# A new order for the 1254 hand-numbered steps of an attention, Fourier and feed-forward kernel

## The chip, the core and the metric

The kernel runs on one core of a Trainium2 chip, in one launch. The metric is the device time of one execution in microseconds (us). Five engines work side by side, each through its own instructions in a fixed order: TensorE (PE; its weight loads are listed as PEld), VectorE (DVE), ScalarE (ACT), GpSimd (POOL) and SyncE (SP). In this kernel SP issues every DMA. An instruction starts when the one ahead of it on its engine has started or ended and the semaphores that it waits for are set, so an instruction that waits holds up everything behind it on that engine.

## The reference

```python
# q, k, v: (4 batches, 12 heads, 448 tokens, 64), float32
scores = cap * np.tanh(q @ k.T / sqrt(64) / cap)        # cap = 30
attn   = exp(scores - max) / (sum(exp(scores - max)) + 1e-9)
x      = (attn @ v), heads side by side: (4, 448, 768)
mixed  = real(fft(fft(x, axis=1), axis=2))              # tokens, then features
u      = x + mixed
un     = (u - mean(u)) / sqrt(var(u) + 1e-6)            # over the 768 features
out    = u + maximum(un @ w_ch1, 0) @ w_ch2             # 768 -> 3072 -> 768
```

## The kernel before, in words

The program is written as small steps, one Python function each; every step issues a handful of instructions. The table `ORDER` gives each step of the first part a number from 1 to 1254, the steps are sorted by it (`at`, `plan.sort`) and issued in that order. Each engine gets its share of that list in the same sequence; the framework puts in the semaphores. So the table sets the order on every engine, SP among them, and nothing reorders it later. A step may not stand ahead of what it needs.

The steps, by what they do:

- **Attention, 48 heads in 24 pairs.** `load_qk` (two DMAs into one of three `qkr` buffers) and `load_v` (into one half of `vt`). `split_q` (DVE) and `split_k` (ACT) round to the high part, `rest_q` and `rest_k` (DVE) make the rest. `scores` (4 or 6 matmuls, L435) fills one of two PSUM tiles `s`; `tanh` (ACT, L445) empties it into one of four tiles `a`; `exp` (ACT, L448) works in place; `weigh` (8 matmuls, L465) multiplies by v. There are 84 tiles of scores and 168 `weigh`. After the seventh `weigh` of a pair, `denominators` and `normalise` (DVE, L479 to L486) put the result into `u`.
- **Fourier transform, once per batch** (`transform`). `fold_tokens`, `fold_features`, `fold_rest` (DVE) and `fold_split` (ACT) use symmetry; `stage1` (12 matmuls, `yps`, L532), `split_y` (ACT), `rest_y` (DVE), `stage2` (18 matmuls, `pq`, L556), `add_u` (DVE, L577 and L581).
- **Layer norm, once per batch.** `moments` (DVE, L590, L591), `rows` (ten small POOL instructions, L599 to L608), `standardise` (four on ACT, L623), `u_cols` (transposes on PE, `pt`, L632), `u_copy` (ACT, into `xc`). `rows_out` (four DMAs, L615) writes two numbers per token to DRAM, four bytes at a time; `row` reads them back over all partitions, for `residual` (DVE).
- **Feed-forward.** `fetch` (DMA) and `weights` (ACT and DVE, three steps a half chunk) make the weights from float64. `operand` (ACT) and `operand_rest` (DVE) split `xc`. A `product` is 6 matmuls: `up` (`ph`, L754, with relu on ACT at every third) or `down` (`po`, L783, added to `xc` by DVE, L792). The hidden layer is worked in 12 groups of 256; the first group (48 products) stands in the table, the other eleven follow in a fixed loop behind it that is not changed.
- **Constants.** `load_constant` and `constant` bring in the cosines and sines.

PSUM tiles `yps`, `pq`, `pt` and every second `po` share two buffers (tag "d"); `av` and the other `po` share one. Here is how a step finds its place:

```python
        i = number[name] = number.get(name, -1) + 1
        t = ORDER[name][i]
        plan.append((t, len(plan), key, f, args, needs))
```

Of the kernel before, what the change touches and what calls it, by code (L numbers as in the profile page):

```python
# [86 lines left out]
        327, 344, 355, 367, 605, 609, 633, 643, 872, 874, 902, 908, 1123, 1126, 1134, 1137  # L87
    ],
    "constant": [
        154, 152, 105, 99, 57, 55, 13, 12  # L90
    ],
    "denominators": [
        60, 103, 148, 185, 236, 280, 338, 375, 411, 473, 517, 558, 619, 651, 691, 743, 791, 828, 891, 918,
        964, 1018, 1055, 1092
    ],
    "exp": [
# [5 lines left out]
    ],  # L102
    "fetch": [
        10, 11, 56, 101, 222, 261, 283, 398, 494, 496, 992, 1007, 1113, 1115
    ],
    "fold_features": [
        158, 161, 195, 198, 291, 294, 437, 440, 489, 493, 569, 572, 687, 689, 753, 756, 839, 841, 929, 932,
        1042, 1045, 1102, 1103
    ],
    "fold_rest": [  # L110
        171, 174, 206, 215, 301, 304, 452, 453, 503, 506, 579, 582, 698, 708, 762, 767, 847, 850, 939, 943,
        1050, 1052, 1106, 1107
    ],
    "fold_split": [
        166, 169, 201, 210, 297, 300, 447, 450, 498, 501, 574, 578, 695, 703, 758, 761, 843, 846, 935, 937,
        1047, 1049, 1104, 1105
    ],
    "fold_tokens": [
        116, 121, 191, 193, 286, 288, 430, 434, 478, 485, 564, 567, 672, 684, 748, 750, 834, 837, 924, 927,
        1031, 1040, 1099, 1101  # L120
    ],
    "load_cap": [
        1
    ],
    "load_constant": [
        108, 104, 61, 59, 15, 14, 3, 2
    ],
    "load_qk": [
        4, 5, 6, 21, 29, 37, 72, 82, 90, 123, 133, 149, 172, 184, 212, 242, 253, 277, 309, 329, 345, 368, 395,
        438, 443, 487, 500, 522, 534, 552, 586, 606, 625, 644, 673, 709, 717, 759, 775, 789, 804, 821, 856,  # L130
        871, 887, 903, 966, 988
    ],
    "load_v": [
        7, 8, 54, 100, 146, 190, 237, 279, 337, 372, 446, 492, 516, 559, 618, 650, 713, 764, 793, 829, 889,
        917, 972, 1017
    ],
    "moments": [
        350, 353, 379, 383, 624, 629, 657, 661, 877, 886, 914, 934, 1127, 1131, 1139, 1140
    ],
    "normalise": [  # L140
        62, 63, 107, 110, 150, 151, 186, 189, 241, 243, 281, 284, 340, 341, 377, 378, 412, 414, 474, 475, 521,
        524, 561, 562, 620, 621, 654, 656, 693, 696, 744, 747, 792, 796, 830, 831, 892, 894, 921, 922, 969,
        976, 1019, 1025, 1065, 1066, 1093, 1098
    ],
    "operand": [
        604, 607, 1067, 1073, 1076, 1091, 1129, 1130, 1132, 1133, 1135, 1136, 999, 1021, 1062, 1190, 1191,
        1192, 1170, 1183, 1193, 1195, 1197, 1198
    ],
    "operand_rest": [
        716, 719, 1071, 1077, 1080, 1094, 1155, 1157, 1159, 1161, 1166, 1169, 1074, 1081, 1084, 1211, 1213,  # L150
        1214, 1231, 1232, 1234, 1235, 1237, 1238
    ],
    "product": [
# [90 lines left out]
    ],  # L244
# [765 lines left out]
```

## Time and profile before

| | us |
|---|---|
| time, median of 3 runs (1073.27 to 1073.58) | 1073.48 |
| span of the profiled execution, first to last instruction | 1064.8 |
| what lies around the span (1073.48 less 1064.8) | 8.7 |
| PE busy | 1017.9 |
| DVE busy | 795.8 |
| ACT busy | 403.9 |
| first matmul starts | 8.5 |
| first group of the feed-forward ends (step 1254) | 415 |

The page gives no total of its own for the profiled execution beyond the span; the 8.7 us are what the timed runs have more. A busy PE is not a PE at its peak: a matmul that streams at half clock is as busy. So the stretches below are read with the column of the granted clock beside the busy time: 1.00 is 2.4 GHz, and 0.50 is 1.2 GHz.

### The profile page before, as it was taken

How to read it: one execution, taken by the hardware profiler on the slowest of the kernel's cores; microseconds unless marked ns; L12 is line 12 of the kernel's file. 1: busy time of each engine (PE TensorE's matmuls, PEld its weight loads, DVE VectorE, ACT ScalarE, POOL GpSimd, SP SyncE). 2: the span in 40 equal slices, each digit the busy share in tenths (PEclk: the TensorE clock that was granted, in tenths of full speed). 3: DMA queues.
4: the chain of work that ended last, by engine and by line, in shares of the span. 5: the costliest groups of instructions: out<-in, count | busy, mean ns of one | idle time of the engine just before them, and what ended most of it. 6: DMA issues, size and time to landing. Idle time of an engine off the chain costs nothing.

```text
span 1064.8 us, 15143 instructions
## 1 busy us (share of the span) xinstructions
PE 1017.9 (96%) x5856; PEld 944.6 (89%) x5856; DVE 795.8 (75%) x1581; ACT 403.9 (38%) x626; POOL 19.2 (2%) x50
## 2 busy tenths in 40 slices
PE   6999899899978789999999999999999999999998
PEld 5899899899877678999999999999999999999997
DVE  5888778668685877777878888787778777777833
ACT  6997797796781411212122221222121222212200
POOL 0000100200100100000000000000000000000000
PEclk9999899999888999999999999999999999999999
DMA  8654763683521010121212212112122122121123
GB/s 222 166 140 108 106 130 87 83 120 94 57 43 47 9 39 17 58 66 48 68 51 62 60 45 69 56 49 60 46 60 60 45 60 59 46 60 54 37 80 129
DMA packets 59239, 77.02 MB, mean 72 GB/s; under 512 B 35616, under 2 KB 40736, under 8 KB 59168
## 3 DMA queue, kind: packets, MB, share of 16 engines
q1 hardware_dynamic: 59168, 76.06, 30.2%
q8 instruction: 46, 0.75, 0.3%
q14 instruction: 25, 0.20, 0.1%
HBM read 70.53 MB, written 5.52 MB: 71 GB/s over the span
## 4 chain that ended last, share of the span: by engine, by line
PE 87%; DVE 4%; ACT 3%; POOL 2%; DMA 2%; issue 1%; SPq 1%; POOLq 0%; ACTq 0%; DVEq 0%
PE ph L754 33%; PE po L783 32%; PE av L465 10%; PE s L435 6%; PE yps L532 3%; PE pq L556 2%; DMA raw<-w1r 1%; ACT u L623 1%; PE pt L632 1%; DVE bs L590 1%; ACT a L445 1%; DVE xc L792 1%; POOL ln L601 0%; DMA qkr<-qkT 0%; SPq L615 0%
## 5 line engine op out<-in xcount | busy, mean ns | idle before, releaser
L783 PE MATMUL po<-hh,w 128*128 128x448 f32 x1728 | 362.9, 368 | 4.5 <-DVE u L577 2.0
L754 PE MATMUL ph<-xs,w 128*128 128x448 f32 x1728 | 359.4, 366 | 3.3 <-DVE xs L327 2.6
L783 PEld LDWEIGHTS po<-hh,w 128*128 128x128 f32 x1728 | 324.6, 189 | 36.6 <-DVE xc L792 4.9
L754 PEld LDWEIGHTS ph<-xs,w 128*128 128x128 f32 x1728 | 323.9, 188 | 31.0 <-DVE xs L327 3.4
L792 DVE TENSOR_TENSOR xc<-xc,po 128x448 f32<-128x448 f32 x288 | 177.2, 618 | 47.3 <-PE po L783 45.4
L465 PEld LDWEIGHTS av<-vt,a 128*114 128x114 f32 x1344 | 153.4, 183 | 8.9 <-ACT a L445 2.0
L465 PE MATMUL av<-vt,a 128*114 128x65 f32 (+1 forms) x1344 | 153.8, 269 | 4.4 <-DVE u L486 1.6
L766 DVE SCALAR_TENSOR_TENSOR hh<-ph,hh 128x448 fp32r<-128x448 f32 x96 | 60.0, 625 | 114.3 <-ACT hh L765 114.3
L667 ACT ACTIVATE wt<-raw 128x384 f32<-128x384 f32 x96 | 53.1, 553 | 229.2 <-DVE w L699 224.7
L765 ACT ACTIVATE hh<-ph 128x448 fp32r<-128x448 f32 x96 | 52.3, 545 | 200.0 <-PE ph L754 200.0
L435 PE MATMUL s<-qhl,khl 128*128 128x452 f32 x384 | 101.6, 399 | 14.0 <-DVE qhl L327 8.5
L322 ACT CAST w<-wt 128x384 fp32r<-128x384 f32 x96 | 48.9, 509 | 121.5 <-DVE wt L674 120.7
L448 ACT ACTIVATE a<-a,capt 128x904 f32<-128x904 f32 x84 | 88.3, 1051 | 1.8
L445 ACT ACTIVATE a<-s,tscale 128x904 f32<-128x904 f32 x84 | 84.6, 1007 | 11.5 <-PE s L435 9.2
L435 PEld LDWEIGHTS s<-qhl,khl 128*128 128x128 f32 x384 | 70.9, 200 | 19.9 <-ACT khl L322 8.5
L674 DVE SCALAR_TENSOR_TENSOR wt<-wt 128x384 f32<-128x384 f32 x96 | 53.6, 558 | 18.3 <-ACT wt L667 8.8
L327 DVE TENSOR_TENSOR wt<-wt,w 128x384 f32<-128x384 f32 x96 | 52.9, 551 | 7.8 <-ACT w L322 7.8
L671 DVE SCALAR_TENSOR_TENSOR wt<-raw,wt 128x384 uint32<-128x384 uint32 x96 | 53.6, 558 | 3.3
L693 DVE SCALAR_TENSOR_TENSOR wt<-raw,wt 128x384 f32<-128x384 uint32 x96 | 53.6, 558 | 3.3
L699 DVE TENSOR_TENSOR w<-wt 128x384 fp32r<-128x384 f32 x96 | 53.6, 558 | 3.4
L532 PE MATMUL yps<-seqT,f 113*128 113x226 f32 (+1 forms) x288 | 38.4, 289 | 4.0 <-DVE f L327 4.0
L532 PEld LDWEIGHTS yps<-seqT,f 113*128 113x128 f32 (+1 forms) x288 | 36.7, 203 | 4.6 <-DVE f L327 4.4
(64 smaller groups left out, 544.9 us busy)
## 6 DMA issues: line engine op xcount, KB each, us to landing
qkr<-qkT SPq DMA_DIRECT2D x96, 226.0 KB, 3.9
raw<-w2r SPq DMA_DIRECT2D x48, 384.0 KB, 3.2
raw<-w1r SPq DMA_DIRECT2D x48, 384.0 KB, 3.1
vt<-vr SPq DMA_DIRECT2D x24, 288.0 KB, 4.4
outT<-xc SPq DMA_DIRECT2D x24, 224.0 KB, 1.9
fraw<-feat SPq DMA_DIRECT2D x6, 193.0 KB, 5.0
dev<-lnrow SPq DMA_DIRECT2D x4, 224.0 KB, 9.5
mean<-lnrow SPq DMA_DIRECT2D x4, 224.0 KB, 3.4
```

Source lines behind the costliest of these rows:

```text
L435: nc.tensor.matmul(ps_t[t][:, i, :SQ], khl[j][:, n, k0 : k0 + P], qhl[:, j], start=((n, j) == terms[0]), stop=((n, j) == terms[-1]),)
L445: nc.scalar.activation(a_t[t], ps_t.pop(t)[:, :, :SQ], AF.Tanh, scale=tscale)
L448: nc.scalar.activation(a_t[t], a_t[t], AF.Exp, scale=capt)
L465: nc.tensor.matmul(pa_t[p][:R, g // 2, o : o + n_ * (D + 1)], a_t[t][:, n, OFF[g] : OFF[g] + R], v, start=u % 7 == 0 and g % 2 == 0, stop= ...
L532: nc.tensor.matmul(ps[:, n * NT2 : (n + 1) * NT2], f[:cnt, ia, 2 * n + c], seqT[n][:cnt, ib, c], start=(k_ == 0), stop=(k_ == 5),)
L671: nc.vector.scalar_tensor_tensor(tu, hi.bitcast(U32), 0xC0000000, tu, op0=ALU.bitwise_and, op1=ALU.bitwise_or)
L674: nc.vector.scalar_tensor_tensor(t, w, HI_MIN, t, op0=ALU.is_ge, op1=mul)
L693: nc.vector.scalar_tensor_tensor(w, lo, 2.0**-52, w, op0=mul, op1=mul)
L754: nc.tensor.matmul(ph[:, :S], w_[:, dc * P : (dc + 1) * P], x_, start=(k_ == 0), stop=(k_ == 3 * NDC - 1),)
L766: nc.vector.scalar_tensor_tensor(hh[:, 1], ph[:, :S], 0.0, f32(hh[:, 0]), op0=ALU.max, op1=sub)
L783: nc.tensor.matmul(po[:, :S], w_[:, dc * P : (dc + 1) * P], hh[:, x_], start=(k_ == 0), stop=(k_ == 3 * GF - 1),)
L792: nc.vector.tensor_tensor(ac, ac, po[:, :S], op=add)
```

## The change

Only the table is changed: each of the 1254 steps gets a new number. No step is added or dropped, no instruction changes its shape, and the loop behind the table is the same. The first list of the table and one that moves far:

```diff
     "load_constant": [
-        108, 104, 61, 59, 15, 14, 3, 2
+        251, 78, 201, 90, 160, 80, 110, 31
     ],
     "rows_out": [
-        402, 404, 449, 457, 677, 680, 722, 728, 946, 949, 975, 994, 1146, 1148, 1164, 1178
+        536, 790, 811, 858, 726, 727, 865, 866, 947, 959, 1007, 1011, 1135, 1137, 1197, 1209
     ],
```

Since the table is written on two lines fewer, every line of the changed kernel behind it has a number lower by two (L435 becomes L433). Three places show what moves.

First, ACT at the start of the program. `khl` is the split keys, `seqT` and `featT` are constants, `a` a tile of scores, `guard` a small constant that needs `cap`. Before:

```order
L362 ACT_TABLE_LOAD
L362 ACTIVATE guard<-ncap 128x1
L322 CAST seqT<-sraw 128x452
L322 CAST featT<-fraw 128x386
L322 CAST khl<-qkr 128x448 x2
L445 ACTIVATE a<-s,tscale 128x904
L448 ACTIVATE a<-a,capt 128x904
```

Now, with what each row waits for:

```order
L320 ACT_TABLE_LOAD [waits DMAHW1_49]
L320 CAST khl<-qkr 128x448 [waits DMAHW0_49]
L360 ACTIVATE guard<-ncap 128x1 [waits DVE_49]
L320 CAST khl<-qkr 128x448 [waits DMAHW4_49,DMAHW3_49]
L443 ACTIVATE a<-s,tscale 128x904 [waits PE_49]
L446 ACTIVATE a<-a,capt 128x904 [waits DMAHW2_49,Activation_49]
```

The two constants left the head of the queue, and the table load, which waited for nothing, now waits for a DMA: the second half of the first head's queries and keys.

Second, ACT around the layer norm of batch 0. `u<-u,ln` is `standardise`, `xc<-pt` is `u_copy`, `a` are the tanh and exp of later scores. Before:

```order
L322 CAST khl<-qkr 128x448
L623 ACTIVATE u<-u,ln 114x768 x4
L322 CAST khl<-qkr 128x448
L667 ACTIVATE wt<-raw 128x384
L322 COPY xc<-pt 128x448 x2
L445 ACTIVATE a<-s,tscale 128x904
L322 COPY xc<-pt 128x448 x2
L448 ACTIVATE a<-a,capt 128x904
L322 COPY xc<-pt 128x448 x2
```

Now:

```order
L621 ACTIVATE u<-u,ln 114x768
L446 ACTIVATE a<-a,capt 128x904
L621 ACTIVATE u<-u,ln 114x768
L320 CAST khl<-qkr 128x448
L443 ACTIVATE a<-s,tscale 128x904
L446 ACTIVATE a<-a,capt 128x904
L320 CAST w_819<-wt 128x384
L443 ACTIVATE a<-s,tscale 128x904
L621 ACTIVATE u<-u,ln 114x768
L443 ACTIVATE a<-s,tscale 128x904
L446 ACTIVATE a<-a,capt 128x904 x2
```

The four `standardise` no longer stand in one block; tanh and exp of later scores stand between them, and the copies of the transposes come later still.

Third, DVE after the last attention pair, where batch 3 is transformed. `den` and `u<-av,den` are `denominators` and `normalise`, `tf` and `ff` the folds, `f` the rest that `stage1` reads, `hh` an instruction that waits for a finished `up` product. Before:

```order
L479 TENSOR_SCALAR den<-av,guard 114x8
L480 RECIPROCAL den<-den 114x8
L486 TENSOR_TENSOR u<-av,den 114x2x128
L327 TENSOR_TENSOR xs<-xc,xs 128x448
L766 SCALAR_TENSOR_TENSOR hh<-ph,hh 128x448
L486 TENSOR_TENSOR u<-av,den 114x2x128
L505 TENSOR_TENSOR tf<-u 114x512
L766 SCALAR_TENSOR_TENSOR hh<-ph,hh 128x448
L505 TENSOR_TENSOR tf<-u 114x512
L511 TENSOR_TENSOR ff<-tf 114x512 x2
L327 TENSOR_TENSOR f<-ff,f 114x512 x2
```

Now:

```order
L477 TENSOR_SCALAR den<-av,guard 114x8
L478 RECIPROCAL den<-den 114x8
L484 TENSOR_TENSOR u<-av,den 114x2x128 x2
L503 TENSOR_TENSOR tf<-u 114x512 x2
L509 TENSOR_TENSOR ff<-tf 114x512 x2
L325 TENSOR_TENSOR y<-yps,y 128x452
L325 TENSOR_TENSOR f<-ff,f 114x512 x2
```

The two rows `hh`, each of which waits for a third `up` product, no longer stand among the folds; the first of them now comes seven rows of this list later, and a `rest_y` stands before the last `f`.

## Rows read from the trace of the kernel before

**Rows 1.** The page, part 1: busy time, share of the span, instructions.

```profile
PE 1017.9 (96%) x5856; PEld 944.6 (89%) x5856; DVE 795.8 (75%) x1581; ACT 403.9 (38%) x626; POOL 19.2 (2%) x50
```

**Rows 2.** Windows by stage: stretch, length, busy by engine, granted clock, DMA share, GB/s.

```profile
8.50:42.80 34.30, 31.07 (x197) 28.76 (x198) 23.21 (x49) 27.86 (x37) 0.00 (x0) 0.95 0.84 219
42.80:79.70 36.90, 36.90 (x300) 35.52 (x298) 33.41 (x70) 33.59 (x47) 0.00 (x0) 1.00 0.57 135
79.70:114.50 34.80, 34.27 (x291) 33.15 (x290) 30.95 (x68) 26.22 (x32) 1.77 (x3) 1.00 0.42 104
114.50:132.80 18.30, 13.97 (x97) 13.36 (x96) 12.46 (x26) 12.86 (x21) 3.26 (x8) 0.81 0.87 109
132.80:194.80 62.00, 61.52 (x507) 59.52 (x507) 49.56 (x105) 50.95 (x64) 1.86 (x3) 1.00 0.47 107
194.80:212.10 17.30, 13.30 (x101) 12.86 (x100) 8.76 (x19) 12.12 (x19) 3.52 (x8) 0.90 0.79 76
212.10:276.30 64.20, 64.20 (x538) 62.58 (x537) 49.09 (x100) 49.82 (x61) 3.54 (x7) 1.00 0.54 95
276.30:307.20 30.90, 23.72 (x149) 21.69 (x148) 20.09 (x45) 23.57 (x35) 0.60 (x4) 0.78 0.69 75
...
318.50:414.90 96.40, 82.30 (x441) 73.10 (x442) 64.73 (x122) 24.29 (x44) 3.60 (x10) 0.95 0.11 27
414.90:1064.80 649.90, 645.94 (x3169) 593.75 (x3167) 489.46 (x952) 129.44 (x251) 0.00 (x0) 1.00 0.20 59
```

**Rows 3.** Chain of waits, pieces of undisturbed PE work: start us, length us, what.

```profile
146.00 1.29 PE s L435 x6
...
153.32 1.56 PE av L465 x16
...
166.85 2.73 PE yps L532 x24
...
248.73 3.59 PE pq L556 x36
...
885.23 14.67 PE ph L754 x72
```

**Rows 4.** Timeline of the start: start us, length us, engine, what, [idle before <-releaser].

```profile
0.71 1.28 ACT L362 ACT_TABLE_LOAD   x1 [0.71 <-PEq L997]
...
7.29 0.57 ACT L322 CAST khl<-qkr 128x448 fp32r<-128x448 f32 x1 [1.61 <-DMA qkr<-qkT]
...
8.50 5.83 PE L435 MATMUL s<-qhl,khl 128*128 128x452 f32 x14 [8.50 <-DVE qhl L327]
```

**Rows 5.** Timeline of the layer norm of batch 0.

```profile
112.57 0.19 POOL L599 COPY ln<-stat 128x4 f32<-128x4 f32 x1 [110.84 <-DVE stat L591]
...
118.29 3.78 ACT L623 ACTIVATE u<-u,ln 114x768 f32<-114x768 f32 x4 [2.75 <-POOL ln L608]
...
122.13 1.76 PE L632 MATMUL pt<-ident,u 113*128 113x113 f32 x8 [3.75 <-ACT u L623]
```

**Rows 6.** DMA issues: what, engine, op xcount, KB each, us from issue to landing.

```profile
qkr<-qkT SPq DMA_DIRECT2D x96, 226.0 KB, 3.9
...
lnrow<-ln SPq DMA_DIRECT2D x8, 0.9 KB, 13.2
```

**Rows 7.** Chain of waits, behind the layer norm of batch 2.

```profile
285.85 13.40 DMA raw<-w1r
```

**Rows 8.** Timeline of PE, behind the same layer norm.

```profile
301.31 1.87 PE L435 MATMUL s<-qhl,khl 128*128 128x452 f32 x4 [4.82 <-ACT a L445]
```

**Rows 9.** Chain of waits where batch 3 is transformed.

```profile
323.25 6.18 PE ph L754 x30
...
333.42 5.46 PE yps L532 x24
...
342.09 1.82 DVE u L577 x2
...
364.20 1.01 PE pt L632 x8
```

More of the change, by code (lines that the diff above doesn't have):

```diff
@@ L86 @@
     "add_u": [
-        327, 344, 355, 367, 605, 609, 633, 643, 872, 874, 902, 908, 1123, 1126, 1134, 1137
+        338, 341, 353, 354, 609, 611, 625, 626, 882, 884, 896, 898, 1106, 1109, 1113, 1114
     ],
     "constant": [
-        154, 152, 105, 99, 57, 55, 13, 12
+        258, 84, 230, 128, 161, 82, 135, 32
     ],
     "denominators": [
-        60, 103, 148, 185, 236, 280, 338, 375, 411, 473, 517, 558, 619, 651, 691, 743, 791, 828, 891, 918,
-        964, 1018, 1055, 1092
+        48, 91, 130, 174, 216, 264, 314, 367, 403, 439, 476, 529, 598, 640, 670, 725, 760, 809, 872, 912, 956,
@@ L95 @@
+        1000, 1037, 1067
     ],
     "exp": [
[5 rows of a table removed]
[5 rows of a table added]
     ],
     "fetch": [
-        10, 11, 56, 101, 222, 261, 283, 398, 494, 496, 992, 1007, 1113, 1115
+        41, 72, 155, 204, 226, 267, 324, 488, 739, 1028, 1049, 1050, 1131, 1246
     ],
     "fold_features": [
-        158, 161, 195, 198, 291, 294, 437, 440, 489, 493, 569, 572, 687, 689, 753, 756, 839, 841, 929, 932,
-        1042, 1045, 1102, 1103
+        169, 151, 232, 187, 283, 290, 414, 451, 523, 457, 565, 539, 664, 663, 734, 740, 832, 834, 924, 919,
@@ L109 @@
+        1030, 1010, 1078, 1076
     ],
     "fold_rest": [
-        171, 174, 206, 215, 301, 304, 452, 453, 503, 506, 579, 582, 698, 708, 762, 767, 847, 850, 939, 943,
-        1050, 1052, 1106, 1107
+        179, 159, 255, 195, 309, 313, 425, 497, 532, 493, 579, 568, 716, 668, 797, 789, 841, 843, 941, 939,
+        1063, 1060, 1088, 1084
     ],
     "fold_split": [
-        166, 169, 201, 210, 297, 300, 447, 450, 498, 501, 574, 578, 695, 703, 758, 761, 843, 846, 935, 937,
-        1047, 1049, 1104, 1105
+        177, 158, 249, 188, 295, 308, 415, 474, 530, 481, 566, 550, 715, 667, 753, 781, 833, 835, 940, 938,
@@ L117 @@
+        1061, 1038, 1081, 1077
     ],
     "fold_tokens": [
-        116, 121, 191, 193, 286, 288, 430, 434, 478, 485, 564, 567, 672, 684, 748, 750, 834, 837, 924, 927,
-        1031, 1040, 1099, 1101
+        109, 121, 182, 186, 277, 282, 375, 383, 453, 456, 534, 535, 650, 652, 732, 733, 815, 816, 917, 918,
+        1003, 1004, 1074, 1075
     ],
     "load_cap": [
-        1
+        7
     ],
     "load_constant": [
-        108, 104, 61, 59, 15, 14, 3, 2
+        251, 78, 201, 90, 160, 80, 110, 31
@@ L127 @@
     ],
     "load_qk": [
[L129 to L131 removed]
+        1, 9, 16, 37, 54, 64, 83, 87, 112, 123, 162, 199, 198, 236, 252, 256, 273, 289, 344, 350, 371, 407, 427,
+        410, 470, 473, 489, 542, 575, 541, 616, 646, 651, 678, 700, 736, 741, 772, 788, 824, 851, 857, 893, 880,
@@ L132 @@
+        932, 951, 967, 999
     ],
     "load_v": [
-        7, 8, 54, 100, 146, 190, 237, 279, 337, 372, 446, 492, 516, 559, 618, 650, 713, 764, 793, 829, 889,
-        917, 972, 1017
+        19, 59, 81, 92, 173, 225, 239, 281, 304, 406, 413, 444, 491, 549, 600, 677, 704, 756, 778, 842, 870,
+        911, 958, 1021
     ],
     "moments": [
-        350, 353, 379, 383, 624, 629, 657, 661, 877, 886, 914, 934, 1127, 1131, 1139, 1140
+        342, 345, 385, 390, 613, 618, 634, 635, 885, 889, 899, 903, 1110, 1111, 1118, 1119
@@ L144 @@
+        1001, 1002, 1041, 1040, 1071, 1069
     ],
     "operand": [
-        604, 607, 1067, 1073, 1076, 1091, 1129, 1130, 1132, 1133, 1135, 1136, 999, 1021, 1062, 1190, 1191,
-        1192, 1170, 1183, 1193, 1195, 1197, 1198
+        831, 612, 1064, 1057, 1086, 1082, 1128, 1130, 1124, 1133, 1138, 1123, 1154, 1100, 1175, 1185, 1193,
+        1189, 1161, 1163, 1168, 1195, 1216, 1187
     ],
     "operand_rest": [
-        716, 719, 1071, 1077, 1080, 1094, 1155, 1157, 1159, 1161, 1166, 1169, 1074, 1081, 1084, 1211, 1213,
@@ L151 @@
-        1214, 1231, 1232, 1234, 1235, 1237, 1238
+        949, 654, 1065, 1062, 1090, 1091, 1129, 1132, 1125, 1136, 1139, 1126, 1180, 1142, 1190, 1188, 1194,
+        1191, 1162, 1165, 1223, 1201, 1217, 1218
     ],
     "product": [
[3 rows of a table removed]
[3 rows of a table added]
     ],
     "residual": [
-        1117, 1121, 1141, 1144, 1149, 1152, 1186, 1199, 1201, 1203, 1205, 1207, 1218, 1219, 1223, 1225, 1227,
-        1229, 1242, 1243, 1247, 1249, 1251, 1253
+        1098, 1101, 1105, 1141, 1134, 1148, 1176, 1158, 1160, 1192, 1198, 1200, 1181, 1183, 1202, 1221, 1226,
@@ L161 @@
+        1224, 1239, 1214, 1240, 1248, 1250, 1231
     ],
     "rest_k": [
-        19, 26, 35, 69, 79, 88, 119, 130, 144, 168, 181, 208, 238, 250, 273, 307, 326, 343, 364, 392, 406,
-        427, 464, 497, 519, 530, 550, 585, 602, 622, 642, 670, 681, 712, 739, 771, 786, 802, 819, 854, 869,
-        884, 899, 950, 973, 979, 1014, 1060
+        5, 12, 25, 45, 69, 71, 105, 127, 144, 153, 191, 213, 221, 241, 266, 305, 336, 334, 364, 380, 397, 428,
+        436, 469, 508, 527, 556, 573, 591, 608, 621, 662, 693, 699, 712, 738, 766, 792, 812, 839, 856, 869, 905,
@@ L166 @@
+        926, 944, 984, 998, 1027
     ],
     "rest_q": [
-        18, 24, 33, 67, 77, 85, 113, 127, 138, 165, 179, 203, 233, 247, 271, 298, 321, 336, 363, 390, 401,
-        425, 462, 482, 514, 529, 546, 576, 601, 616, 639, 668, 679, 704, 736, 768, 781, 799, 816, 852, 867,
-        882, 897, 945, 960, 965, 1012, 1057
+        3, 13, 23, 39, 58, 67, 100, 116, 143, 150, 190, 209, 234, 238, 276, 303, 337, 326, 355, 373, 388, 426,
+        432, 466, 504, 498, 553, 567, 583, 599, 636, 666, 686, 698, 706, 755, 776, 786, 806, 830, 853, 874, 909,
@@ L171 @@
+        923, 965, 987, 993, 1031
     ],
     "rest_y": [
-        211, 217, 252, 256, 315, 317, 468, 499, 533, 537, 595, 597, 732, 774, 783, 808, 860, 863, 952, 958,
-        1061, 1069, 1114, 1119
+        229, 214, 312, 285, 318, 330, 471, 514, 577, 511, 587, 580, 748, 718, 820, 836, 849, 860, 966, 979,
+        1089, 1083, 1099, 1094
     ],
     "row": [
-        1108, 1110, 1162, 1210
+        1095, 1115, 1169, 1213
     ],
     "rows": [
-        388, 666, 941, 1143
+        394, 648, 914, 1127
@@ L198 @@
-        879, 893, 920, 967, 971, 1008, 1026
+        4, 10, 24, 44, 60, 70, 102, 124, 140, 152, 166, 200, 220, 240, 261, 288, 332, 327, 363, 376, 396, 409,
+        434, 463, 506, 526, 546, 560, 590, 597, 620, 647, 682, 691, 710, 737, 765, 780, 805, 825, 855, 867, 904,
+        925, 943, 955, 989, 1016
     ],
     "split_q": [
-        16, 22, 31, 64, 74, 83, 111, 124, 136, 163, 177, 202, 227, 245, 265, 296, 320, 333, 360, 387, 399,
-        416, 461, 480, 512, 527, 545, 575, 599, 615, 637, 665, 675, 701, 734, 760, 778, 797, 814, 844, 866,
@@ L203 @@
-        881, 895, 944, 955, 962, 1010, 1056
+        2, 11, 22, 38, 57, 66, 99, 115, 134, 149, 163, 203, 217, 237, 274, 302, 319, 325, 349, 372, 387, 424,
+        431, 450, 499, 496, 552, 558, 582, 596, 617, 655, 685, 695, 705, 746, 775, 785, 798, 826, 852, 863, 901,
+        922, 964, 985, 990, 1025
     ],
     "split_y": [
-        197, 207, 232, 248, 312, 314, 465, 481, 523, 532, 589, 592, 729, 752, 779, 805, 858, 861, 948, 954,
-        1059, 1064, 1112, 1116
+        219, 211, 301, 284, 311, 328, 464, 513, 561, 510, 586, 576, 747, 717, 819, 823, 848, 859, 963, 975,
@@ L208 @@
+        1080, 1073, 1097, 1093
     ],
     "stage1": [
-        187, 200, 228, 239, 305, 310, 458, 471, 515, 525, 583, 588, 724, 746, 772, 795, 851, 857, 942, 947,
-        1053, 1058, 1109, 1111
+        184, 172, 272, 223, 310, 317, 452, 509, 555, 503, 581, 571, 742, 703, 808, 803, 847, 854, 960, 970,
+        1079, 1072, 1096, 1092
     ],
     "stage2": [
-        318, 324, 335, 352, 598, 603, 610, 617, 864, 870, 875, 878, 1120, 1122, 1125, 1128
+        331, 335, 346, 352, 593, 604, 615, 619, 873, 877, 883, 890, 1103, 1104, 1108, 1112
@@ L229 @@
+        1166, 1172, 1174, 1184
     ],
     "u_copy": [
-        420, 421, 428, 431, 439, 442, 697, 700, 706, 710, 720, 723, 974, 977, 983, 985, 995, 997, 1165, 1168,
-        1174, 1179, 1180, 1185
+        480, 484, 492, 501, 547, 595, 696, 697, 721, 773, 796, 864, 981, 995, 1005, 1014, 1068, 1070, 1156,
+        1159, 1167, 1173, 1182, 1186
     ],
     "weigh": [
[9 rows of a table removed]
[9 rows of a table added]
     ],
     "weights": [
-        49, 53, 71, 93, 97, 131, 139, 220, 224, 229, 258, 262, 266, 276, 308, 322, 394, 407, 418, 444, 448,
@@ L247 @@
-        454, 470, 509, 591, 991, 996, 1001, 1003, 1006, 1020, 1023, 1027, 1032, 1037, 1046, 1124, 1171, 1181,
-        1187, 1194, 1196
+        42, 52, 63, 79, 107, 108, 156, 192, 193, 205, 242, 243, 257, 279, 296, 320, 442, 443, 477, 495, 505,
+        515, 569, 690, 799, 1023, 1026, 1033, 1044, 1046, 1171, 1196, 1199, 1225, 1229, 1235, 1236, 1241, 1245,
+        1247, 1251, 1252
     ],
```

14 lines of the change are left out of this document (5 added, 9 removed), and 52 rows, old and new, of the table ORDER.

## The prediction

> **What bounds the kernel now.** I read the busy times first: PE is busy for 1017.9 of 1064.8 us, the next engine, DVE, for 795.8 [rows 1]. So PE sets the time, and a new order can win only what PE loses. That is read from a table by stage [rows 2]: in each stretch, length less PE busy is idle, and one less the granted clock is the share of the time in which the array ran at 1.2 instead of 2.4 GHz. I add both (time that was idle and at the lower clock is then counted twice, so this is on the high side; a half-clock matmul counts as busy, so the idle alone would be too low).
>
> - before the first matmul: 8.50 [rows 4]
> - 8.5 to 42.8 (first 12 score tiles): 3.23 idle + 0.05 x 34.3 = 4.9
> - 114.5 to 132.8 (layer norm of batch 0): 4.33 + 0.19 x 18.3 = 7.8
> - 194.8 to 212.1 (batch 1): 4.00 + 0.10 x 17.3 = 5.7
> - 276.3 to 307.2 (batch 2): 7.18 + 0.22 x 30.9 = 14.0
> - 318.5 to 414.9 (batch 3 and the first products): 14.1 + 0.05 x 96.4 = 18.9
> - the four quiet stretches between these, 197.9 us in all: 36.9, 34.8, 62.0 and 64.2 us hold 0.0, 0.53, 0.48 and 0.0 idle at full clock, 1.0 together
> - from 414.9 on: 4.0 idle, most of it behind the last matmul.
>
> So about 60 us of the first 415 are lost, nearly all in five places. Behind 414.9 PE streams 72 matmuls in 14.67 us without a break [rows 3]; the loop there is not changed, and I give it no change.
>
> The quiet stretches show that an order can keep PE full. They also show the room: from 42.8 to 79.7 ACT is busy for 33.6 and DVE for 33.4 of 36.9 us [rows 2], so an order that puts more of their work ahead would make them the bound.
>
> **The change part by part.** The work is the same, so each edit costs or saves only waits.
>
> *Queries ahead of constants.* Before, the first cast of keys starts at 7.29, after 1.61 us of waiting for its DMA, and the first matmul at 8.50 [rows 4]. Now the load is the first DMA and issues at about 0.7 instead of 2.1, and no constant is in front of it. By the median of its kind, 3.9 us [rows 6], its second half (issued 0.6 later) lands at about 5.2. But the table load (1.28 us, [rows 4]) now waits for that DMA, where before it was over by 2.0. So the cast starts at 6.5, ends at 7.1, and the matmul starts near 7.2; the DVE steps for the queries (about a microsecond, in the shade of the table load) are done by then. Gain 1.3. Bounds: the landing takes 5.2 us, as from issue to cast before: no gain; or 3.9 and no wait: 1.6.
>
> The trace has one table load, 1.28 us, with nothing waiting behind it [rows 4]. The Trainium skill, "ScalarE: Activation LUTs", section "What ACT_TABLE_LOAD costs", gives 1283 ns for the load, which agrees, and a drain of about 1380 ns with it, which no run here shows. By that page the cast would start at 7.9 and the start would lose 0.1 instead of gaining 1.3, an estimate from its figure.
>
> For the next 35 us ACT is the tightest (27.9 of 34.3 busy before, [rows 2]). By a count of the steps its work up to the twelfth tile stays the same: two constants fewer, one tanh more. What can go is its 6.4 of idle; with the matmuls 1.3 earlier and the keys of each head cast just ahead of use, I count 2.8 of the 4.9 back; bounds 0 and 4.9.
>
> *Layer norm and transposes spread.* In batch 0 the chain from the first POOL instruction (112.57) to the first transpose (122.13) takes 9.6 us, 3.78 of it `standardise` in one block [rows 5]. What covers it is the PE work between the last `moments` and the first `u_cols`. One `weigh` is 0.78 us (16 matmuls in 1.56), a tile of scores 0.86 or 1.29, a `stage1` 1.37, a `product` 1.22 [rows 3]. By count of the steps:
>
> - batch 0: before 5 `weigh` and 2 tiles, 6.0; now 17 `weigh`, 7 tiles, 1 `stage1`: 21.1
> - batch 1: before the same, 6.0; now 9 `weigh`, 4 tiles: 10.9
> - batch 2: before 3 `weigh`, 2 tiles, 2 `stage1`: 7; now 13 `weigh`, 5 tiles, 2 `stage1`: 17.6
> - batch 3: before 5 `product`, 6.1; now 10: 12.2.
>
> All four are now longer than the chain. The cost is on ACT: four `standardise` between the exps make the later exps late, by about 1 us each, and in batch 1 the cover is only 1.3 longer than the chain while the exps wait behind it. I leave 2.0 lost in batch 0 and 1.5 in batch 1. Gains 7.8 - 2.0 = 5.8 and 5.7 - 1.5 = 4.2. Bounds: half of each, or all.
>
> *The DMAs of batch 2.* Four-byte writes (`rows_out`) take 13.2 us to land where a load of queries takes 3.9 [rows 6], and what is issued behind them waits too: one `fetch` 13.40 [rows 7], so that PE stood for 4.82 us before a score tile [rows 8]. Now the weights that this fetch brought are used among the products of batch 1, and in this place only one weight load stands behind the writes. Of the four writes of batch 2, two stand singly among the loads; the other two stand together, ahead of the last load of v, which by the count of PE steps has 12 us from its release to its use. I leave 2 lost of 14.0: gain 12. Bounds: the two pairs still cost what rows 8 show, gain 7; or all, 14.
>
> *Batch 3 among the first products.* Two waits. Before, the last `up` product of batch 0 ends at 329.43 (323.25 + 6.18) and `stage1` starts at 333.42: 4.0 idle, since `normalise` and the folds stood on DVE behind two instructions `hh` that wait for products; then 24 `yps` took 5.46 instead of 2.73 at half clock [rows 3, 9]. 6.7 in all. Now DVE does `normalise` and the folds first, 5 us for the chain (seven instructions of 0.4 to 0.7 and one on ACT), while PE has two `stage1` and two products: 2.73 + 2.44 = 5.2. I count 6 of 6.7 back. Then from the first `add_u` (342.09) to the first transpose (364.20) there are 22.1 us of DVE, POOL and ACT in series [rows 9]; PE had three `stage2` (1.80 each, [rows 3]) and six products, 12.7, so 9.4 were lost. Now three `stage2` and 13 products stand beside the same chain, 21.3, and a weight step is taken out of the chain. I leave 2: gain 7.5. Sum 13.5; bounds 7 and 16. What is late next: residuals and conversions put off to the end, on DVE, that have 5 us of slack by my count.
>
> *Sum.* 1.3 + 2.8 + 5.8 + 4.2 + 12 + 13.5 = 39.6. Against it I put 4 us for waits in the quiet stretches, which the new order refills and for which I have no row: a choice, a tenth of the gain. 1064.8 - 35.6 = 1029.2 of span; with the 8.7 around it, the same as before, 1037.9: I say 1038.
>
> **The rivals.**
>
> - *All of it comes* (A). Upper bounds: 1.6 + 4.9 + 7.8 + 5.7 + 14 + 16 = 50, no new wait: 1023. For it: three quiet stretches of 1.0 loss in 198 us. Against: the first stage is bound by ACT, and every layer norm still has a chain in series.
> - *Half of it is given back* (B). ACT and DVE are 90% busy in the fullest stretch, and tanh, exp and conversions now take turns with `standardise` and `u_copy`; several tiles even change places (tile 41 before 40). If each of ten pieces of the order costs 2 us of waiting, 20 of 39.6 remain: 1054.
> - *Slower* (C), one mechanism: the loads of queries behind the four-byte writes. There are now writes in seven places among the attention steps, once three in a row, and at one point head 29 is loaded before 27 and keeps one of three buffers for long. If a write holds PE up as in rows 8, 4.82, and the lower clock that followed there costs its share again (0.22 x 30.9 = 6.8 for two waits in that stretch, [rows 2], so 3.4), each place costs 8.2. Seven: 57, against 39.6: 1091. It decides from five places on. Against it: of six such places before, one held PE up; and by the count of PE steps most loads behind the writes now have 10 us or more until their use.
> - *No change* (D): the gains and C cancel, 1073.5.
>
> **How the numbers follow.** Forecast, 1029 to 1047: 0.50. A, under 1029: 0.17. B, 1047 to 1071: 0.22. D: 0.03. C: 0.08. This kernel's measurement can tell 0.2%, 2.1 us, from no change: faster 0.89, same 0.03, slower 0.08. The range leaves out the 0.08 of C, 0.03 of D, and the ends of A and B: 1021 to 1059.
>
> **What would show it.** First matmul near 7.2 with the table load behind its DMA. The first 12 tiles done by 39, the 24th by 74 to 75 (79.7 before). No stretch of half clock around the first transposes of batches 0 to 2. `stage1` of batch 3 at full clock, 2.7 for 24. Step 1254 ends near 380 instead of 415, and the span from there is 650 as before. I am wrong if PE waits for `qkr` loads behind `lnrow` writes, if the quiet stretches lose more than 5 us, or if DVE at the end holds back the last products.

## The result and the profile after

The changed kernel takes 1028.33 us (median of 4 runs, 1025.68 to 1029.74) against 1073.38 (4 runs, 1066.82 to 1073.58) for the kernel before: a ratio of 0.9597, 95% interval 0.9561 to 0.9633. Forecast were 1038, in a range of 1021 to 1059. The profiled execution has a span of 1027.5 us (forecast 1029.2) at a granted clock of 0.997.

The page, part 1, answers to [rows 1]:

```profile
PE 1003.1 (98%) x5856; PEld 931.8 (91%) x5856; DVE 792.4 (77%) x1581; ACT 397.1 (39%) x626; POOL 19.3 (2%) x50
```

With the same 5856 matmuls PE is busy 14.8 us less: fewer of them ran at half clock. The span is 37.3 shorter, so the other 22.5 were PE's idle time.

The table by stage (length, busy by engine, granted clock, DMA share, GB/s). The first two cuts are those of [rows 2], the 12th and the 24th tile of scores; the later ones are places of the changed kernel, since its steps stand in another order:

```profile
7.10:37.70 30.60, 30.60 (x222) 28.27 (x223) 24.06 (x55) 28.33 (x39) 0.00 (x0) 1.00 0.98 225
37.70:73.00 35.30, 35.30 (x283) 34.14 (x282) 32.80 (x72) 33.15 (x48) 0.00 (x0) 1.00 0.72 177
...
104.30:114.70 10.40, 10.40 (x89) 10.11 (x87) 8.03 (x19) 9.78 (x13) 3.89 (x10) 1.00 0.54 131
114.70:179.90 65.20, 65.20 (x550) 63.48 (x548) 56.27 (x117) 55.23 (x76) 5.03 (x10) 1.00 0.44 101
179.90:186.10 6.20, 6.20 (x48) 5.95 (x48) 5.32 (x12) 6.20 (x9) 0.00 (x0) 1.00 1.06 126
186.10:216.20 30.10, 30.10 (x247) 29.22 (x247) 18.25 (x39) 27.10 (x37) 0.00 (x0) 1.00 0.84 101
216.20:230.90 14.70, 12.64 (x91) 12.16 (x90) 8.84 (x16) 9.08 (x14) 0.00 (x0) 0.88 0.52 101
...
254.30:282.00 27.70, 22.28 (x167) 20.47 (x166) 12.75 (x27) 18.25 (x26) 0.00 (x0) 0.94 1.00 74
282.00:301.20 19.20, 16.26 (x138) 15.34 (x137) 12.54 (x27) 13.06 (x19) 0.00 (x0) 1.00 0.23 58
301.20:377.70 76.50, 73.53 (x410) 65.52 (x409) 67.44 (x130) 26.56 (x51) 4.15 (x10) 1.00 0.11 28
377.70:1027.50 649.80, 645.85 (x3170) 593.69 (x3168) 492.85 (x959) 130.32 (x253) 0.00 (x0) 1.00 0.21 60
```

In the first six rows, which hold the first 24 tiles and the layer norms of batches 0 and 1 (but for the last transpose of batch 1, at 230.61), PE is busy for the whole length at full clock; so it is in the two stretches left out. From the first POOL instruction to the first transpose there are now 20.0, 11.3 and 18.7 us in batches 0, 1 and 2 (108.08 to 128.11, 171.64 to 182.90, 247.25 to 265.92 in the timelines), and PE waits before none of these transposes. Beside the start and the end, losses stand in three places: 216 to 231, 254 to 301, and 3.0 among the first products. With the prediction's own rule (idle, and length times what the clock lacks) the ledger reads, in us lost:

| place | before | after | gain | forecast |
|---|---|---|---|---|
| before the first matmul | 8.5 | 7.1 | 1.4 | 1.3 |
| first 12 tiles | 4.9 | 0.0 | 4.9 | 2.8 |
| layer norm of batch 0 | 7.8 | 0.0 | 7.8 | 5.8 |
| layer norm of batch 1 | 5.7 | 0.0 | 5.7 | 4.2 |
| layer norm of batch 2, to the first product | 14.0 | 7.1 + 2.9 | 4.0 | 12 |
| batch 3 and first products | 18.9 | 3.0 | 15.9 | 13.5 |
| quiet stretches | 1.0 | 3.8 | -2.8 | -4 |
| the long loop | 4.0 | 4.0 | 0 | 0 |
| sum | 64.8 | 27.9 | 36.9 | 35.6 |

The sum agrees with the 37.3 of the span (the prediction's list leaves out 307.2 to 318.5, 0.6 idle before; with it the gain is 37.5). That the forecast of the span came so near is partly luck: one term that was 8 too large stood beside four that were 1.5 to 2.4 too small.

The start, from the timeline of all engines (start, length, engine, what, [idle before <- releaser]); it answers to [rows 4]:

```profile
0.72 1.21 SPq L401 DMA_DIRECT2D qkr<-qkT  x2
...
5.15 1.28 ACT L320 ACT_TABLE_LOAD   x1 [5.15 <-DMA qkr<-qkT]
...
6.44 0.56 ACT L320 CAST khl<-qkr 128x448 fp32r<-128x448 f32 x1
...
7.06 2.16 PE L433 MATMUL s<-qhl,khl 128*128 128x452 f32 x4 [7.06 <-ACT khl L320]
```

Load first, the table load behind its landing, the cast behind the table load, the matmul at 7.06. The cast starts 0.01 us after the table load ends. The Trainium skill, "ScalarE: Activation LUTs", section "What ACT_TABLE_LOAD costs", puts a drain of about 1380 ns beside the load at every switch to a different set; in this place no such time is in the trace, and the measurement decides.

What PE waited for after that, from its timeline (the rows with a wait over 1 us, up to the last score tile):

```profile
225.04 2.43 PE L530 MATMUL yps<-seqT,f 112*128 112x226 f32 x12 [2.06 <-DVE f L325]
...
276.70 1.88 PE L433 MATMUL s<-qhl,khl 128*128 128x452 f32 x4 [4.55 <-ACT a L443]
...
285.93 2.61 PE L463 MATMUL av<-vt,a 128*114 128x65 f32 x24 [1.17 <-ACT a L446]
```

Behind the first two the granted clock is at half, as windows on these stretches show:

```profile
225.50:228.90 3.40, 3.40 (x15) 3.22 (x15) 0.83 (x2) 1.37 (x3) 0.00 (x0) 0.50 0.02 1
276.70:280.10 3.40, 3.40 (x13) 3.11 (x14) 3.26 (x9) 3.40 (x5) 0.00 (x0) 0.50 1.67 28
```

PE names ACT, so the next view is the timeline of ACT in that place:

```profile
262.04 0.57 ACT L320 CAST khl<-qkr 128x448 fp32r<-128x448 f32 x1 [2.41 <-DMA qkr<-qkT]
...
275.17 0.56 ACT L320 CAST khl<-qkr 128x448 fp32r<-128x448 f32 x1 [5.72 <-DMA qkr<-qkT]
...
284.36 0.56 ACT L320 CAST khl<-qkr 128x448 fp32r<-128x448 f32 x1 [3.68 <-DMA qkr<-qkT]
```

ACT stands for the queries and keys of the last three heads (45 to 47). The timeline of SP shows what those loads were issued among:

```profile
204.14 3.75 SPq L613 DMA_DIRECT2D lnrow<-ln  x2
208.00 1.11 SPq L401 DMA_DIRECT2D qkr<-qkT  x2
...
252.04 0.32 SPq L613 DMA_DIRECT2D lnrow<-ln  x1
252.54 1.11 SPq L401 DMA_DIRECT2D qkr<-qkT  x2
...
258.00 0.59 SPq L613 DMA_DIRECT2D lnrow<-ln  x1
258.69 6.11 SPq L401 DMA_DIRECT2D qkr<-qkT  x4
264.84 0.96 SPq L613 DMA_DIRECT2D lnrow<-ln  x2
```

and the chain of waits that ends at 302 how long some of them took, the one issued at 208.5 (ahead of the wait of `yps`) among them:

```profile
208.51 12.22 DMA qkr<-qkT
...
253.07 8.87 DMA qkr<-qkT
...
264.21 20.05 DMA qkr<-qkT
```

These took 8.9 to 20 us. Of the 96 loads the trace gives a landing to eight: the five that stand away from writes took 3.4 to 4.3 us, the three near writes (issued at 184.06, 213.52 and 252.54) 8.5 to 10.8. SP was held as well: its four issues from 258.69 took 6.11 us. On DVE the load issued at 208.51 shows in the queries of that head, which come late ahead of the folds that `yps` waits for:

```profile
220.85 0.40 DVE L322 CAST qhl<-qkr 128x452 fp32r<-128x452 f32 x1 [2.61 <-DMA qkr<-qkT]
```

That is the mechanism of rival C, in three waits and for less than it was priced.

The chain where batch 3 is transformed answers to [rows 9]:

```profile
303.82 2.91 PE yps L530 x24
306.73 1.23 PE ph L752 x6
307.96 3.59 PE pq L554 x36
...
328.08 4.89 PE ph L752 x24
332.98 0.79 PE pt L630 x8
```

`stage1` runs at full clock, 2.91 for 24 matmuls (5.46 before), and the transposes stand directly behind products.

### The profile page after: what moved, and what is told of

Its sections match the earlier page's. It is cut to its first block, busy times and chain, and to the rows that moved or that the text cites. A ratio compares the mean times of both kernels' runs of the same rounds, so it can differ in the third digit from the quotient of the medians.

```text
span 1027.5 us, 15133 instructions
## 1 busy us (share of the span) xinstructions
PE 1003.1 (98%) x5856; PEld 931.8 (91%) x5856; DVE 792.4 (77%) x1581; ACT 397.1 (39%) x626; POOL 19.3 (2%) x50
## 4 chain that ended last, share of the span: by engine, by line
PE 91%; DMA 4%; DVE 2%; ACT 1%; SPq 1%; POOL 0%; issue 0%; DVEq 0%; ACTq 0%; POOLq 0%
PE ph L752 34%; PE po L781 34%; PE av L463 10%; PE s L433 7%; DMA qkr<-qkT 4%; PE pq L554 3%; PE yps L530 3%; PE pt L630 1%; SPq L613 0%; DVE bs L588 0%; SPq L401 0%; DVE hh L764 0%; DVE xc L790 0%; ACT khl L320 0%; ACT hh L763 0%
## 5 line engine op out<-in xcount | busy, mean ns | idle before, releaser
L463 PEld LDWEIGHTS av<-vt,a 128*114 128x114 f32 x1344 | 147.7, 180 | 6.0 <-ACT a L446 2.8
L463 PE MATMUL av<-vt,a 128*114 128x65 f32 (+1 forms) x1344 | 149.0, 265 | 2.8 <-ACT a L446 1.9
L433 PE MATMUL s<-qhl,khl 128*128 128x452 f32 x384 | 98.3, 391 | 12.6 <-ACT khl L320 7.1
L443 ACT ACTIVATE a<-s,tscale 128x904 f32<-128x904 f32 x84 | 84.3, 1013 | 18.9 <-PE s L433 16.5
L433 PEld LDWEIGHTS s<-qhl,khl 128*128 128x128 f32 x384 | 69.5, 195 | 19.4 <-ACT khl L320 7.1
L672 DVE SCALAR_TENSOR_TENSOR wt<-wt 128x384 f32<-128x384 f32 x96 | 53.6, 558 | 13.5 <-ACT wt L665 3.4
```

The costliest lines, as they stand in the source:

```text
L433: nc.tensor.matmul(ps_t[t][:, i, :SQ], khl[j][:, n, k0 : k0 + P], qhl[:, j], start=((n, j) == terms[0]), stop=((n, j) == terms[-1]),)
L443: nc.scalar.activation(a_t[t], ps_t.pop(t)[:, :, :SQ], AF.Tanh, scale=tscale)
L463: nc.tensor.matmul(pa_t[p][:R, g // 2, o : o + n_ * (D + 1)], a_t[t][:, n, OFF[g] : OFF[g] + R], v, start=u % 7 == 0 and g % 2 == 0, stop= ...
L672: nc.vector.scalar_tensor_tensor(t, w, HI_MIN, t, op0=ALU.is_ge, op1=mul)
```

## The experiments

All are edits of the table of step times. The first seven start from the changed kernel (1028.33, 0.9597), the last three concern the kernel before. Edits are shown in an equivalent, shorter form. Ratios are to the kernel before, with 95% intervals; profiles are named by the kernel. An entry of `rows_out` is the place of one DMA that writes four bytes at a time. The changed kernel was timed in one set only, beside a kernel before of 1073.38; the three later sets have 1069.94, 1070.85 and 1070.51 for the kernel before. Differences to the changed kernel below subtract medians of different sets; worked out from the ratios instead they move by up to some 2 us (`w_all` 11.8 instead of 13.3), so small ones are weak.

**1. `w_all`: the writes of batches 0 and 2 put behind the loads they stood among.**

```diff
+ORDER["rows_out"][1], ORDER["rows_out"][2] = 857.1, 857.2
+ORDER["rows_out"][8:12] = [1028.1, 1028.2, 1028.3, 1028.4]
```

> The new order with six of its twelve small writes of layer-norm rows moved behind the loads of queries that they held up: two of batch 0 from behind the load of head 38 to behind that of head 41, all four of batch 2 behind the last loads of queries and v. In the trace of the new order PE stands for 2.1, 4.6 and 1.2 us at 223, 271 and 285 us, and runs at 1.2 GHz for 6.8 us behind the first two, because casts of keys wait for loads that took 9 to 20 us to land. Theory W (the writes cause it): these waits go, 12 to 15 us less than the new order, 1013 to 1017. Rival (the loads are late by themselves, because three buffers are too few or they are issued late): under 3 us of change, 1025 to 1028.

Measured: 1015.00 (1014.01 to 1015.38), ratio 0.9487 [0.9471, 0.9503], span 1013.1, clock 1.000. Its page, and all that PE waited for (us in total, times, longest):

```profile
PE 999.2 (99%) x5856; PEld 930.2 (92%) x5856; DVE 792.2 (78%) x1581; ACT 397.0 (39%) x626; POOL 19.3 (2%) x50
```

```profile
PE s L439 <- ACT khl L326: 6.9, 1, 6.9
PE po L787 <- DVE xc L796: 2.3, 3, 0.9
PE po L787 <- DVE hh L770: 0.6, 3, 0.2
```

All waits behind attention loads are gone and so is the half clock: 3.9 less busy time and 10.5 less idle are the 14.4 of span. The writes cost the changed kernel 13.3 us in the median, 14.4 in the two profiles. In `cap_first` below, which has the same moves, the loads with a known landing that were issued at 216.90 and 248.36 took 3.4 and 5.1 us (one at 230.51, behind the five writes that now stand together, 7.7).

**2. `w_b2` and 3. `w_b0`: the same for one batch each.** `w_b2` has the second line of the edit above alone, `w_b0` the first.

> The new order with only the four writes of batch 2 moved behind the last loads of queries and v. Theory W: the waits at 271 and 285 us go (4.6 and 1.2 us of standing, some 3 of half clock, and the late weights behind them), the one at 223 stays: 8 to 11 us less than the new order, 1017 to 1020. Rival: the writes of both batches act together through a queue that is never emptied; then either half alone gives less than 3 us.

> The new order with only two writes of batch 0 moved from behind the load of head 38 to behind that of head 41. Theory W: the wait of 2.1 us at 223 and its 3.4 us at half clock go, 3 to 4 us less than the new order, 1024 to 1026; together with the other half it must come to what both gave, 13.3. Rival: as for the other half, under 1 us.

Measured: `w_b2` 1015.63 (1015.41 to 1017.72), ratio 0.9483 [0.9452, 0.9513], 12.7 less; `w_b0` 1025.32 (1023.58 to 1027.59), 0.9568 [0.9541, 0.9596], 3.0 less. `w_b0` is as expected, but its runs overlap with those of the changed kernel (1025.68 to 1029.74); its profile no longer has the wait of `yps`. In `w_b2` PE is busy for 45.64 of the 45.70 us from 254.3 to 300.0, at full clock. It gave more than expected, since in its profile the wait of `yps` at 225, which the writes of batch 0 were to own, is 0.7 as well:

```profile
PE yps L534 <- DVE f L329: 0.7, 1, 0.7
```

The parts sum to 15.7, both together give 13.3: that wait differs from execution to execution, and how much of it is due to the writes of batch 0 stays open. So does whether a load suffers from the writes ahead of it, from those issued within a microsecond behind it, or from its own late issue on SP (two writes at 204.14 held SP for 3.75 us; four issues of loads take 6.11 among the writes and 2.78 in the last such group of `w_all`): no run parted them.

**4. `ln_block`: `standardise` and the transposes of batches 0 to 2 back in a block, where the cover is.** `t0` to `t2` are the places of the last `weigh` steps before the first transposes.

```diff
+for b, (t0, t1, t2) in enumerate(((416, 419, 420), (658, 659, 665), (933, 936, 937))):
+    for g in range(4):
+        ORDER["standardise"][4 * b + g] = t0 + 0.1 + g / 100
+    for p in range(6):
+        ORDER["u_cols"][6 * b + p] = (t0, t1, t2)[p // 2] + 0.5 + p % 2 / 10
+        ORDER["u_copy"][6 * b + p] = (t0, t1, t2)[p // 2] + 0.55 + p % 2 / 10
```

> The new order with the layer norm of batches 0, 1 and 2 put back into a block: four standardise in a row and the six transposes right behind, with as much PE work between the last moments and the first transpose as before (5 to 7 us). Theory S (the spread hides a chain of 9.6 us): each batch loses 4 to 8 us again with a stretch at 1.2 GHz, 12 to 20 more than the new order, 1040 to 1048. Rival (what the batches lost before came from other steps of the old order): within 3 us of the new order.

Measured: 1050.73 (1049.87 to 1051.87), ratio 0.9826 [0.9805, 0.9846], 22.4 more than the changed kernel, somewhat over what was expected. The timeline around the layer norm of batch 0 has the wait of [rows 5] back:

```profile
113.11 3.78 ACT L629 ACTIVATE u<-u,ln 114x768 f32<-114x768 f32 x4 [0.85 <-POOL ln L614]
...
116.95 1.15 PE L638 MATMUL pt<-ident,u 113*128 113x113 f32 x8 [4.05 <-ACT u L629]
```

and PE's list of waits has it three times:

```profile
PE pt L638 <- ACT u L629: 12.2, 3, 4.1
```

Half clock follows behind each of the three (3.4 to 6.8 us long); two more such stretches stand behind waits of 1.63 (`yps`) and 4.61 (scores), of the kind that the changed kernel has too. So the spreading, not something beside it, is what pays in the layer norms. It is worth more here than the 13.5 that the ledger gives batches 0 and 1, and batch 2, which is undone too, was not tried by itself.

**5. `hh_first`: the folds of batch 3 back behind two `hh`.**

```diff
+ORDER["normalise"][46:48] = [1069.91, 1069.1]
+for i, t in ((4, 1069.2), (5, 1069.4)):
+    ORDER["operand"][i], ORDER["operand_rest"][i] = t, t + 0.1
+ORDER["product"][:6] = [1069.6, 1069.7, 1069.8, 1074.1, 1074.2, 1074.3]
+ORDER["fold_tokens"][22:24] = [1074.05, 1074.4]
```

> The new order with the six up products of batch 0 put ahead of the last folds of batch 3 again, and one normalise and one fold behind the DVE instructions that wait for these products, as before. Theory F: the folds come 4 to 5 us late, the stage1 behind them runs at half clock, and four products fewer stand beside the chain from add_u to the transposes: 8 to 12 us more than the new order, 1036 to 1040. Rival (PE has other work and the place does not matter): within 2 us of the new order.

Measured: 1038.15 (1036.35 to 1040.92), ratio 0.9707 [0.9683, 0.9731], 9.8 more, as expected. PE's timeline shows the wait, and the 24 matmuls at half clock again, as in [rows 9]; the second row is the other half of the edit, the products that no longer stand beside the chain:

```profile
311.69 5.43 PE L537 MATMUL yps<-seqT,f 112*128 112x226 f32 x24 [3.11 <-DVE f L332]
...
332.33 7.55 PE L788 MATMUL po<-hh,w 128*128 128x448 f32 x24 [3.08 <-DVE xc L797]
```

**6. `const_first`: the cap and the two constants loaded ahead of the queries again.**

```diff
+ORDER["load_cap"][0], ORDER["scales"][0] = 0.1, 1.1
+ORDER["load_constant"][7], ORDER["load_constant"][6] = 0.2, 0.3
+ORDER["constant"][7], ORDER["constant"][6] = 1.2, 1.3
```

> The new order with cap and two constants loaded and split ahead of the first queries again, as before; the table load again waits for nothing. Theory Q: the first matmul moves from 7.1 to 8.5 us, and ACT, which sets the pace of the first tiles, has two casts more ahead of tile 12 by its place in the order but none more in all: 1 to 3 us more than the new order, 1029 to 1031. Rival (ACT has slack enough to hide it): 0, 1028.

Measured: 1029.88 (1028.42 to 1031.11), ratio 0.9627 [0.9609, 0.9645], 1.55 more. The ranges of the two kernels overlap, so by time alone it is not parted from no change; the profile has the effect at the start, with the first matmul at 8.6 instead of 7.1:

```profile
PE s L438 <- DVE qhl L330: 8.6, 1, 8.6
```

From there on nothing is lost: from 8.6 to 39.2, which hold the first 12 tiles, PE is busy for 30.60 of 30.60 us at full clock. So what the new order wins in the first 12 tiles does not hang on the queries standing first.

**7. `cap_first`: `w_all`, and the cap alone ahead of the queries,** so that the table load waits for nothing.

```diff
 # with the edit of w_all
+ORDER["load_cap"][0], ORDER["scales"][0] = 0.1, 1.1
```

> Both moves of the writes, and the load of cap with the five small DVE steps on it ahead of the first queries, so that the table load waits for nothing. Theory T (the table load behind the first DMA costs its 1.28 us): the first cast starts at the landing, 1.3 less 0.45 for the issue of cap: 0.8 us less than with the writes alone, 1014.2, first matmul at 6.3. Rival (the first tiles are paced by ACT and PE at the low clock anyway): 1015.0, no change in the end though the first matmul is earlier.

Measured: 1014.53 (1013.93 to 1014.78), ratio 0.9465 [0.9443, 0.9487]. That is 0.5 under `w_all` with overlapping ranges. The table load starts at 0.72 and is out of the way, but the first matmul is no earlier; the timeline of the start says why:

```profile
5.88 0.40 DVE L329 CAST qhl<-qkr 128x452 fp32r<-128x452 f32 x1 [1.08 <-DMA qkr<-qkT]
6.31 0.63 DVE L332 TENSOR_TENSOR qhl<-qkr,qhl 64x452 fp32r<-64x452 f32 x1
...
7.08 2.44 PE L440 MATMUL s<-qhl,khl 128*128 128x452 f32 x5 [7.08 <-DVE qhl L332]
```

Two instructions on DVE are as long as the table load's wait was, and the queries land 0.7 later. That the table load costs anything at the start is not shown. This and `w_all` are the fastest versions; both beat the two kernels of the case.

**8. `before_again`: the kernel before, unchanged,** to see where its spread comes from (1066.54 to 1075.86 over all sets).

> The kernel before, unchanged, profiled again. All runs so far took 1.8 us more than their own span, not 8.7, so the first profiled execution must have been one of the shorter ones, near 1066.6. Theory: a longer execution differs in a few long waits for DMA landings behind the small writes, not evenly over the program. Rival: a constant longer time around the span.

Measured: 1069.58 (8 runs, 1066.54 to 1071.33), ratio 0.9987 [0.9965, 1.0009]. Its profiled execution has a span of 1068.4 against 1064.8. The two agree within half a microsecond up to the 75th tile; then comes the place of [rows 8], with another length, and half clock around it for 13.7 instead of 6.8 us:

```profile
302.38 1.87 PE L435 MATMUL s<-qhl,khl 128*128 128x452 f32 x4 [7.44 <-ACT a L445]
```

```profile
298.20:311.90 13.70, 9.52 (x40) 9.19 (x41) 10.79 (x21) 9.62 (x14) 0.00 (x0) 0.50 0.20 43
```

The wait behind the four-byte writes is 4.82 in one execution and 7.44 in the other.

**9. `before_w2`: in the kernel before, the four writes of batch 2 put behind the last loads.**

```diff
+ORDER["rows_out"][8:12] = [1017.1, 1017.2, 1017.3, 1017.4]
```

> The old order with one change: the four writes of batch 2 moved behind the last load of v. Theory W: the long wait before the scores at 296 to 301 us goes with its half clock, 5 to 10 us less than before (1060 to 1065 where before takes 1070), and since that wait is what differs between executions, the runs lie closer together. Rival (the fetch of weights is late because its buffer comes free late): under 2 us.

Measured: 1065.16 (9 runs, 1060.61 to 1068.06) against 1070.51, ratio 0.9944 [0.9922, 0.9966]: 5.4 less, as expected. PE's waits for `a` fall from 5.4 in the first profile of the kernel before to 2.1 (in an execution that is the shortest of its nine):

```profile
PE s L439 <- ACT a L449: 2.1, 2, 1.6
```

But its runs lie 7.5 apart, no closer than before. These writes alone do not make the spread, and the next run shows another place: its order is the same up to batch 3, yet its profiled execution stays at half clock from 38.0 to 47.8, where the kernel before was at 1.00, and comes to the first transpose at 127.03 instead of 122.13. Ahead of that half clock none of the sixteen writes has been issued (the first at 122.09).

**10. `before_fold`: in the kernel before, the last `normalise` and the folds of the third part of batch 3 ahead of the first `hh`,** nothing else.

```diff
+ORDER["normalise"][47] = 1093.5
+ORDER["fold_tokens"][22:24] = [1094.1, 1094.2]
+ORDER["fold_features"][22:24] = [1094.3, 1094.4]
+ORDER["fold_split"][22:24] = [1094.5, 1094.6]
+ORDER["fold_rest"][22:24] = [1094.7, 1094.8]
```

> The old order with one change: in batch 3 the last normalise and the folds of the third part stand ahead of the two DVE instructions that wait for up products, as in the new order. Theory F: the 4.0 us before stage1 and the half clock behind them (2.7) go, 4 to 7 us less than before, 1063 to 1066 where before takes 1070. Rival (the series from add_u to the transposes behind it sets the end of this part whatever comes before): under 2 us.

Measured: 1062.79 (6 runs, 1060.61 to 1068.22), ratio 0.9936 [0.9913, 0.9959]: 7.7 less, where the wait and the half clock of [rows 9] were put at 6.7. The chain (of an execution that is the longest of its six) has `stage1` at full clock, without a step of DVE ahead of it:

```profile
328.99 6.23 PE ph L761 x30
335.22 2.67 PE yps L539 x24
```

## Why the prediction was right, point by point

*What bounds it.* Right: PE set the time, and only what PE loses moved. The rule counted 64.8 us lost before, and by it 36.9 of the 37.3 gained are accounted for.

*Queries ahead of constants.* Right in each step: first matmul at 7.06 (forecast 7.2), behind the table load. Undoing it moves the first matmul by 1.5 in the profile (`const_first`). That the table load is what the start waits for holds for this order; `cap_first` shows that without its wait DVE's two steps end as late.

*First 12 tiles.* Right in direction, too small: all 4.9 came back, not 2.8, and the 12th tile ends at 37.7 (39 forecast), the 24th at 73.0 (74 to 75). ACT was busy 28.3 of 30.6 us there and did not hold PE up. Of the two reasons given, matmuls that start 1.3 earlier are not it, since `const_first` starts as late as the kernel before and loses nothing there; keys that are cast just ahead of use were not tried by themselves. Before, PE had stood twice, for 1.60 us at 23.60 and here:

```profile
37.81 2.67 PE L465 MATMUL av<-vt,a 128*114 128x130 f32 x24 [1.63 <-DVE u L486]
```

The chain of waits in front of this row runs over casts of the constants `seqT` and `featT` on ACT to `normalise` on DVE. The new order has neither wait; which of its moves took them away no run shows. So the cause of this term is open.

*Layer norms of batches 0 and 1.* Right: cover longer than the chain. The chain itself got longer than 9.6 (20.0 and 11.3), about as long as the cover that was counted (21.1 and 10.9), without a wait. The 2.0 and 1.5 set aside for late exps were not needed; `ln_block` shows the mechanism by taking it back.

*The DMAs of batch 2.* This step failed: 12 forecast, 4.0 measured, under the lower bound of 7. The transposes themselves wait no longer. But the prediction took the writes to stand among loads with late use, and counted 12 us from release to use for only one of them. In the trace SP issues the loads of heads 45 to 47 from 252 to 265, among the four writes, and their casts on ACT came 2.4, 5.7 and 3.7 late. The wait moved from a load of weights [rows 7] to loads of keys. `w_b2` gives 12.7 for these writes, about what the step had claimed. This was one of the prediction's own signs of being wrong, PE held up by loads of queries behind the writes; the time came out near all the same because other terms were too small.

*Batch 3 among the first products.* Right, and near the upper bound: 15.9 against 13.5, no wait before the transposes, `stage1` at full clock. `before_fold` shows the fold's part by itself, 7.7. `hh_first` undoes both parts, 9.8: in its profile 5.8 at `stage1` (3.11 of waiting, 5.43 instead of 2.73) and some 4.6 at the `down` products further on (3.08 and 7.55, against 0.87 and 5.15 in the changed kernel).

*The allowance of 4 in the quiet stretches.* 2.8 net of the 1.0 that was lost before, all of it in one stretch (216 to 231), where a load issued behind two writes at 204 came late.

*The time around the span.* Wrong: 8.7 was the difference between the profiled execution and the median of others. In all runs that list a span it is 1.7 to 2.2 (1029.28 against 1027.5). The execution profiled before was a short one: 1064.8 of span belongs to a time near 1066.8, the lowest of its four. That is why the median fell by 45 when the two profiles differ by 37.3, and why 1038 was 10 too high with the span right to 1.7.

*Rivals.* B and D fell. Of A nearly all came, except batch 2. C was right as a mechanism and wrong in number and price: three waits from the writes of two batches, 13.3 us in all instead of 8.2 for each of seven places.

## What to carry to other kernels

Where one engine sets the time, write down what it loses by place, and put beside every serial chain more work of that engine than the chain is long; a chain cut into pieces among other work cost PE nothing here as long as this held. Put small scattered writes where no load with a near use is issued beside them, and count for every load among them, not for the last one only, the time from its issue to its use. Compare span with span, and look at the spread of the runs before adding what lies around one profiled execution.

## What the runs showed that had not been expected

- Loads issued among four-byte writes took 8.9, 12.2 and 20.05 us to land, where five away from them took 3.4 to 4.3. Six such writes (0.9 KB each by [rows 6]) are worth 13.3 of 1028 us (11.8 by the ratios). Not every load near a write costs something: the one issued at 184.06, behind two writes, took 10.8 us, and PE did not wait.
- With them out of the way (`w_all`, `cap_first`) runs lie within 1.4 us of each other, where the changed kernel's spread over 4.1 and those of the kernel before over up to 8.2 in one set. That the writes make the spread is not shown: these are four or five runs each, the runs of `ln_block`, which has the writes in place, lie within 2.0, and `before_fold` has another place that differs.
- A single wait of 2.06 us left 3.4 us of half clock behind it, and one of 4.55 the same; the wait of 1.17 at 285.93 and those of up to 0.9 at the products left none.
